# Two Hedgehog stages in one list-scheduled order, PSUM banks given singly, four VectorE passes moved

## The chip, the cores and the metric

The kernel runs on one NeuronCore of a Trainium2 chip. A core has five engines that run side by side, each with its own queue in program order: TensorE (PE, matrix products; its weight loads are listed apart as PEld), VectorE (DVE), ScalarE (ACT), GpSimd (POOL) and SyncE (SP, which here only issues DMAs). They wait for each other on semaphores. Products land in PSUM, 8 banks of 128 x 512 fp32 values. The metric is device time in microseconds, the median of several executions.

## The reference

Four layers on a sequence of 2048 rows of 512, with 32 heads of 16: attention, Hedgehog, attention, Hedgehog, each behind a layer norm and with a residual.

```python
def _A_ref(x, wqkv, wo):
    q, k, v = ...            # x @ wqkv, split in heads
    p = _softmax(einsum("bhqd,bhkd->bhqk", q, k) * Dh ** -0.5)
    return merge(einsum("bhqk,bhkd->bhqd", p, v)) @ wo

def _B_ref(x, wqkv, w_phi, wo):
    q, k, v = ...
    pq, pk = q @ w_phi, k @ w_phi                      # per head
    phi_q = concatenate([_softmax(pq), _softmax(-pq)])  # 32 features
    phi_k = concatenate([_softmax(pk), _softmax(-pk)])
    kv, z = phi_k^T v, sum(phi_k)
    o = (phi_q kv) / (phi_q z + 1e-6)
    return merge(o) @ wo

x = x + _A_ref(_layernorm(x), A_wqkv, A_wo)
x = x + _B_ref(_layernorm(x), B_wqkv, B_w_phi, B_wo)
x = x + _A_ref(_layernorm(x), A_wqkv, A_wo)
x = x + _B_ref(_layernorm(x), B_wqkv, B_w_phi, B_wo)
```

## The kernel before

Everything is one program of straight code. Rows are taken in 16 tiles of 128 (`tt`), four of which are a block `j` of 512. Numbers are held as pairs of fp16 (a high part and a rest), so that a product is three passes (`PASSES`) and a projection of a tile is 12 matmuls of 128 x 512. A layer norm leaves its result transposed in `xnT`.

*Attention* (`LayerA.attention`) is scheduled by a planner of its own, exponentials on ACT being the bound. Its last rows, the third output chunk of block 3 with its residual and layer norm, are a generator, `last_tail`, kept in `self.fill`.

*The feed of a Hedgehog layer* (`LayerB.feed`, called per block at the end of `attention`) is written out by hand. For each tile PE projects keys (`pk`), queries (`pq`) and values (`pbv`), with the transposes of the query features of the tile before (`turn`, L1918) and the key-value product of the tile before (`gather`, L1925) between them. `expo` makes the features' exponents: on VectorE the maximum and minimum per head (L1867, L1868) and two subtractions (L1870, L1871) read PSUM, then ACT takes the exponential (L1872). `part_sums` sums and inverts (L1878, L1879) and scales the keys' inverse by `KS` (L1881), all on VectorE; GpSimd multiplies (L1887). `halves` makes the fp16 pair of the keys (ACT L1893, GpSimd L1894). The values' high part comes from ACT (L1837), their rest from VectorE:

```python
low = lambda: nc.vector.scalar_tensor_tensor(
    vt[:, 1, :, 0:16], pvh, 2.0 ** -8, vt[:, 0, :, 0:16], op0=ALU.mult, op1=ALU.subtract)
```

Steps of `last_tail` are pumped in between the tiles (`self.pumps`), three after each of the first four, then one at a time: L751 (`po`), L754, the layer norm with L561, the transposes L645 (`pst`).

*The flow* (`LayerB.flow`) begins when `blocks` has copied the key-value sums out of PSUM. It is ordered by a list scheduler, `Flow`: tasks are generators that yield an engine and an assumed duration, and the earliest possible one goes next, by rank among those that are due. The ranks of stages and blocks are tables (`RANKS`, and `TAIL` in the last layer). Tasks are `heads` (products L2076, ACT copy L2089, VectorE transposes and division L2095 to L2112, GpSimd rest L2117), `out_block` (L2137, residual add L2140), and, if an attention layer follows, `norm_in` (layer norm), `project` (keys and queries of the next layer's first octet, evacuated by L2234, L2237, L2240), `values` and `bounds` (norm products L1219 and the bound row, `sh`, that the first scores need). A task takes PSUM as a pair of banks (`S` or `W`), or as a single bank of two (`M`).

The attention layer's scores are L1358, and its first one in the second attention layer ends the first Hedgehog stage.

Of the kernel before, what the change touches and what calls it, by code (L numbers as in the profile page):

```python
# [50 lines left out]
GAP = -2  # L51
# [10 lines left out]
RANKS = dict(query=(2,) * 4, heads=(12.4, 3.3, 24, 30.4), out=(10.2, 17.5, 30.6, 25.2), ln=(2.3, -16.8, 14.2, 5.8),  # L62
             keys=(29.8, 57, 32.4, 34.4), project=(59.7, 22.9, -4.7, 53.4), values=(56.3, 0.5, 50, 57.4))
TAIL = dict(query=(5,) * 4, heads=(4.6, 26.6, 16.2, 25.9), out=(11.1, 5.6, 11.5, 25.9))
SOON = ()
# [22 lines left out]

PASSES = ((0, 0), (1, 0), (0, 1))
# [3 lines left out]
def mha_hedgehog_stack(ctx, tc, x_in, a_wqkv, a_wo, b_wqkv, b_wphi, b_wo, out, shmin=SHMIN):  # L93
# [46 lines left out]
    def make_bones():  # L140
        for u in range(4):
            nc.vector.tensor_reduce(bo32[:, u, 8 * u:8 * u + 8], ident.rearrange("p (h d) -> p h d", d=DH), AX.X, ALU.add)
        nc.vector.tensor_copy(bones, bo32)

# [388 lines left out]
    class Norm:  # L533
# [148 lines left out]
        def steps(self):  # L682
            for t in range(4):
                yield
                self.turned(t, 1, psum1("pst").unsqueeze(1))
                if t < 2:
                    self.scaled(t + 2)
            return self.xnT

# [31 lines left out]
    def o_block(j, ob, wo, co, x_src, x_dst, box, after=None, wide=True, early=False, cs=range(NC4)):  # L721


        def load(t2):
# [3 lines left out]
            return xt  # L728

        xt2 = [] if wide else [load(0), load(1)]  # L730
        for t2 in range(2):
            r = (4 * j + 2 * t2) * P
            xt = load(t2) if wide else xt2[t2]
            if wide:
                ps2 = banks("po2")
# [6 lines left out]
            for u in range(0 if early and t2 == 0 else 2):  # L742
                t = 2 * t2 + u
                n = 0
                for c in cs:
                    for a, b in PASSES:
                        if not wide or n % 4 == 0:
                            yield None if n or u + t2 == 0 else GAP
                        if n == 0:
                            ps = ps2[:, u, :] if wide else psum1("po")  # L750
                        nc.tensor.matmul(ps, ob[c][:, a, t * P:(t + 1) * P], wo[:, b, c, :], start=(n == 0), stop=(n == 3 * len(cs) - 1))  # L751
                        n += 1
                if not wide:
                    nc.vector.scalar_tensor_tensor(xt[:, u, :], ps, co, xt[:, u, :], op0=ALU.mult, op1=ALU.add)  # L754
            if wide:
                nc.vector.scalar_tensor_tensor(xt, ps2, co, xt, op0=ALU.mult, op1=ALU.add)
# [126 lines left out]
    class Flow:  # L883

        def __init__(self, **free):
            self.clock = {"T": 0.0, "V": 0.5, "A": 0.5, "P": 0.0}
            self.free, self.tasks, self.count, self.end = free, [], 0, 0.0

        def add(self, gen, rank, ready=0.0):
# [4 lines left out]
            self.pull(t)  # L894

        def pull(self, t):

            while True:
                try:
                    need = next(t.gen)  # L900
                except StopIteration:
                    self.tasks.remove(t)
                    return
                if need[0] == "until":
# [6 lines left out]
                if t.last is not None and t.last != need[0]:  # L911
                    t.ready += 0.25 if t.last == "T" else 0.08
# [10 lines left out]
        def take(self, *names):  # L923
            name = min((name for name in names if self.free[name]), key=lambda name: min(self.free[name]))
            self.free[name].remove(min(self.free[name]))
            return name

        def give(self, name, n=1, wait=0.1):
            self.free[name] += [self.end + wait] * n

        def run(self):

            while self.tasks:
                for t in sorted(self.tasks, key=lambda t: (t.rank, t.seq)):
                    if t.cond is not None:
                        at = t.cond()
                        if at is not None:
                            t.cond, t.ready = None, max(t.ready, at)
                            self.pull(t)
                best = None  # L940
                for e, c in self.clock.items():
                    mine = [t for t in self.tasks if t.need is not None and t.need[0] == e]
                    if not mine:
                        continue
                    due = [t for t in mine if t.ready <= c + HOLD]
                    t = min(due, key=lambda t: (t.rank, t.ready, t.seq)) if due else min(mine, key=lambda t: (t.ready, t.rank, t.seq))
                    at = max(c, t.ready)
# [3 lines left out]
                self.end = self.clock[t.need[0]] = at + t.need[1]  # L951
                t.ready, t.last = self.end, t.need[0]
                t.need = None
                self.pull(t)

    class LayerA:
# [173 lines left out]
        def norm_task(self, G, idx, acc):  # L1130
# [30 lines left out]
            elif j < NJ - 1:  # L1161
                self.more(self.tail(j, dst))
            else:
                self.last = dst
# [4 lines left out]
        def values0(self, j, ps):  # L1169
# [9 lines left out]
            dst = q["v"][:, j * 528:(j + 1) * 528].rearrange("p (x e) -> p x e", e=33)[:, :, 1:33]  # L1179
# [32 lines left out]
        def head_norms(self, i):  # L1212

            psn = psum1("psn")
# [3 lines left out]
            for n, (u, sq) in enumerate(us):  # L1218
                nc.tensor.matmul(psn[0:32, :], bones[:, u], sq, start=(n == 0), stop=(n == len(us) - 1))  # L1219
            nc.vector.tensor_reduce(self.oct[0]["nm"][0:32, i:i + 1], psn[0:32, :], AX.X, ALU.max)  # L1220
# [59 lines left out]
        def head_values(self, j):  # L1280
            self.values0(j, psum1("pv_"))
# [206 lines left out]
        def last_tail(self, j, ob):  # L1488
            xts = []
            ln = Norm(xts, f"a{self.li}_{j}")  # L1490
            yield from o_block(j, {3: ob}, self.wo, con["oA"], self.x_dst, self.x_dst, xts, ln.half, wide=False, cs=(3,))
            for _ in ln.steps():
                yield GAP
            self.out.append(ln.xnT)

# [971 lines left out]
```

## Time and profile before

| | us |
|---|---|
| three runs | 2444.0, 2450.16, 2451.32 |
| median | 2450.16 |
| the profiled execution | 2445.7 |
| its span | 2443.9 |
| first Hedgehog stage: feed, flow | 987.4 to 1163.9, 1163.9 to 1291.0 |
| second Hedgehog stage: feed, flow | 2192.2 to 2366.0, 2366.0 to 2443.9 |
| granted TensorE clock, mean | 0.99 |

In the rows of the profile a time is the start from the beginning of the span, and the number behind it a duration. Durations of neighbouring instructions of an engine overlap by some tens of ns, so that differences of starts are the better price of a row of them. In square brackets stands how long the engine was idle before, and what ended that.

### The profile page before, as it was taken

Reading aid. Unit: us, or ns where it says so; the run is one execution under the profiler, and the core shown is the slowest. Engines: PE = TensorE matmul, PEld = TensorE weight load, DVE = VectorE, ACT = ScalarE, POOL = GpSimd, SP = SyncE. Lnnn points to the kernel's source line nnn. Section 1 sums busy time; section 2 is a strip of 40 time slices with the busy share of each in tenths; the row PEclk is TensorE's granted clock in tenths of the full one; section 3 lists DMA queues with packets and bytes.
Section 4 is the critical chain, followed back from the end, with each engine's and each line's share of the span. In section 5 each row is a group of like instructions: output and inputs, shape, how many; then the busy total and the mean of one; then the engine's idle time right before and its main releaser. Section 6 shows DMA issues by size and latency. Waiting matters only on the chain. (4 is left out here: it accounts for less than half of the span.)

```text
span 2443.9 us, 115599 instructions
## 1 busy us (share of the span) xinstructions
PE 2285.6 (94%) x52586; PEld 1203.6 (49%) x52586; DVE 1900.5 (78%) x3007; ACT 2076.5 (85%) x2323; POOL 326.0 (13%) x476
## 2 busy tenths in 40 slices
PE   6999999999999999889898999999999999998998
PEld 4455555545545554445345554555455444444543
DVE  8567656988786876889974788788978785579897
ACT  6899999999999999444548999999999999984453
POOL 3000000000000000366440000000000000006552
PEclk9999999999999999999999999999999999999999
DMA  5410431233135522010123003303311621210003
GB/s 186 80 22 8 90 64 30 41 44 60 47 78 129 165 89 68 32 35 19 61 72 56 18 19 45 43 4 47 46 49 25 129 86 50 78 65 27 27 1 114
DMA packets 160573, 143.66 MB, mean 59 GB/s; under 512 B 70488, under 2 KB 137672, under 8 KB 159176
## 3 DMA queue, kind: packets, MB, share of 16 engines
q1 hardware_dynamic: 158888, 133.40, 23.1%
q8 instruction: 413, 6.77, 1.2%
q0 software_dynamic: 1184, 2.77, 0.3%
q14 instruction: 88, 0.72, 0.1%
HBM read 62.16 MB, written 41.94 MB: 43 GB/s over the span
## 5 line engine op out<-in xcount | busy, mean ns | idle before, releaser
L1358 PE MATMUL s<-kq 49*32 49x512 f16 x14688 | 771.9, 381 | 65.8 <-DMA kq<-sh 4.5
L1358 PEld LDWEIGHTS <-kq 49*32 49x32 f16 x15872 | 381.0, 89 | 691.8 <-issue 571.4
L1805 PEld LDWEIGHTS <-xnTa 128*128 128x128 f16 x1152 | 110.6, 99 | 157.9 <-DVE f L1871 30.8
L1887 POOL TENSOR_TENSOR f<-f,su 128x1024 f32<-128x1024 f32 x58 | 112.2, 1934 | 492.5 <-DVE su L1881 478.3
L1119 POOL PARTITION_ALL_REDUCE nma<-nmx x6 | 6.3, 1057 | 990.3 <-DVE nmx L1116 990.3
L1364 ACT ACTIVATE p__1008<-s 128x1024 f32<-128x1024 f32 x119 | 127.8, 1074 | 2.9 <-PE s L1358 2.7
L1364 ACT ACTIVATE p__27549<-s 128x1024 f32<-128x1024 f32 x114 | 122.3, 1073 | 2.8 <-PE s L1358 2.6
L1364 ACT ACTIVATE p__27547<-s 128x1024 f32<-128x1024 f32 x109 | 116.9, 1072 | 7.5 <-PE s L1358 7.4
L1364 ACT ACTIVATE p__1011<-s 128x1024 f32<-128x1024 f32 x114 | 122.4, 1074 | 0.0
L1364 ACT ACTIVATE p__27550<-s 128x1024 f32<-128x1024 f32 x112 | 120.2, 1073 | 0.9 <-PE s L1358 0.8
L1364 ACT ACTIVATE p__27548<-s 128x1024 f32<-128x1024 f32 x112 | 120.4, 1075 | 0.3 <-PE s L1358 0.2
L1364 ACT ACTIVATE p__27553<-s 128x1024 f32<-128x1024 f32 x112 | 120.4, 1075 | 0.0
L1364 ACT ACTIVATE p__1007<-s 128x1024 f32<-128x1024 f32 x110 | 118.0, 1073 | 1.3 <-PE s L1358 1.0
L1364 ACT ACTIVATE p__1010<-s 128x1024 f32<-128x1024 f32 x110 | 118.3, 1075 | 0.7 <-PE s L1358 0.6
L1364 ACT ACTIVATE p__1009<-s 128x1024 f32<-128x1024 f32 x108 | 116.3, 1077 | 1.8 <-PE s L1358 1.8
L1364 ACT ACTIVATE p__1013<-s 128x1024 f32<-128x1024 f32 x108 | 115.9, 1074 | 1.3 <-PE s L1358 1.2
L1364 ACT ACTIVATE p__1012<-s 128x1024 f32<-128x1024 f32 x109 | 116.7, 1071 | 0.2
L1872 ACT ACTIVATE f<-f,c_pB 128x1024 f32<-128x1024 f32 x62 | 70.1, 1148 | 51.9 <-DVE f L1871 51.6
L1805 PE MATMUL pbv<-wbv,xnTa 128*128 128x512 f16 x384 | 91.6, 390 | 24.0 <-DVE f L1871 23.9
L1364 ACT ACTIVATE p__1006<-s 128x1024 f32<-128x1024 f32 x103 | 110.8, 1076 | 2.1 <-PE s L1358 1.9
L1364 ACT ACTIVATE p__27552<-s 128x1024 f32<-128x1024 f32 x104 | 111.6, 1073 | 0.3
L1364 ACT ACTIVATE p__27551<-s 128x1024 f32<-128x1024 f32 x104 | 111.4, 1072 | 0.1
(671 smaller groups left out, 7187.0 us busy)
## 6 DMA issues: line engine op xcount, KB each, us to landing
kq<-stg SPq DMA_DIRECT2D x168, 128.0 KB
xd<-xt SPq DMA_DIRECT2D x112, 128.0 KB
xt<-xd SPq DMA_DIRECT2D x80, 128.0 KB
xt<-xd SPq DMA_DIRECT2D x20, 512.0 KB
v<-vyt SPq DMA_DIRECT2D x384, 16.0 KB
oD<-osp SPq DMA_DIRECT2D x48, 128.0 KB
ob<-oD SPq DMA_DIRECT2D x48, 128.0 KB
xd<-xt SPq DMA_DIRECT2D x12, 512.0 KB
```

The costliest lines, as they stand in the source:

```text
L1119: nc.gpsimd.partition_all_reduce(mm, m, P, bass_isa.ReduceOp.max)
L1358: nc.tensor.matmul(banks2[u][32 * c:32 * c + 32, :], self.side(g, half, 64 * u, 0, kt * P + 32 * c, 32), self.side(g, half, 64 * u, 1, j * ...
L1364: nc.scalar.activation(pt, s, AF.Exp, scale=EXPS)
L1805: nc.tensor.matmul(dst, xnT[:, a, c, t * P:(t + 1) * P], w(b, c), start=(i == 0 and c == 0), stop=(i == 2 and c == NC4 - 1))
L1872: nc.scalar.activation(f, f, AF.Exp, scale=con["pB"])
L1887: nc.gpsimd.tensor_tensor(f3, f3, self.part_sums(f3, slice(0, 64), factor), ALU.mult)
```

## The change

The hand-written feed, the pumped tail and the flow become one `Flow` a Hedgehog stage. `attention` ends with its last product; it hands over what its engines still have to do (`self.left`) and the PSUM of its last group (`self.closing`).

- `Flow` keeps eight PSUM banks. A task names what it needs in its step (`"one"` bank, `"two"` neighbours, a buffer), and gets it when the step is placed (`near`, `pick`). Between two steps of a task there is a table of latencies by engines (`LAG`) instead of two numbers.
- `closing` (the last group's normalisation), `tail_out` (the third output chunk of block 3) and `norm_in` for that block are tasks. `key`, `value` and `query` are tasks of a tile, ranked by 9.45 per tile with lags for values, queries and the tail (`LAGS`).
- Four passes leave VectorE: the scaling by `KS` goes to ACT; the values' rest goes to GpSimd, for which ACT first copies the projection to SBUF (`vh2`); the epsilon of the division becomes a bias of the ACT copy of the head products (`con["eps"]`); the evacuation `tq` of the next layer's keys and queries goes to ACT, and its upper clamp to the VectorE pass that follows.
- In the closing, the copy out of PSUM and the fp16 cast go to ACT, the rest to GpSimd. The layer norm's first estimate `y` has a stride of two. The last layer's last output half is added and sent in two pieces, and the order of loads on SP moves with the tasks.

```diff
-RANKS = dict(query=(2,) * 4, heads=(12.4, 3.3, 24, 30.4), out=(10.2, 17.5, 30.6, 25.2), ln=(2.3, -16.8, 14.2, 5.8),
+RANKS = dict(heads=(19.2, -43.8, 20.1, 9.9), out=(50.3, 46.2, 35.8, 25.9), ln=(24.4, -17.8, -49.2, 43.1),
...
+LAGS = (11.7, 21.1, 47), (19.8, 26.5, 34.9)
+TILE = 9.45
...
+    def near(self, wants):
+        at = 0.0
+        for name in wants:
+            if name == "one":
+                x = min(self.banks)
+            elif name == "two":
+                x = min(max(self.banks[b:b + 2]) for b in (0, 2, 4))
+            else:
+                x = min(self.free[name], default=FAR)
+            at = max(at, x)
+        return at
...
-            with tc.manual_schedule(engines=COMPUTE):
-                for j in range(NJ):
...
-                    nxt.feed(j, self.out[j], lambda t: self.pumps(3 if t < 4 else t > 4))
+            self.left = {"T": 0.0, "V": max(0.0, plan.clock["V"] - pe), "A": max(0.0, act - pe), "P": max(0.0, plan.clock["P"] - pe)}
...
+            def key(tt):
+                yield known(blocks, (j, t // 2))
+                b = yield "T", 2.6, "one"
+                project(one(b), tt, lambda b, c: self.wqk[:, 1, b, c, :])
+                f, f3, su = yield from features(one(b), b)
...
+                yield "A", 0.2
+                nc.scalar.activation(su, su, AF.Copy, scale=KS)
...
+                    yield "P", 1.9
+                    nc.gpsimd.tensor_tensor(f3, f3, su.unsqueeze(2).to_broadcast([P, 64, DH]), ALU.mult)
+                    yield "A", 0.97, "p"
+                    nc.scalar.activation(fk[:, 0, :], ff, AF.Copy)
+                    yield "P", 2.08
+                    nc.gpsimd.tensor_tensor(fk[:, 1, :], ff, fk[:, 0, :], ALU.subtract)
...
+                yield known(values, tt)
+                yield "T", 0.74
...
+            def value(tt):
+                    yield "A", 0.5, "yb"
+                    nc.scalar.activation(vh.rearrange("p h d -> p (h d)"), one(b), AF.Copy, scale=2.0 ** -8)
+                    F.give_bank(b)
+                    vt = (yield "A", 0.45, "dep", "vt").tile
+                    nc.scalar.activation(vt[:, 0, :, 0:16], vh, AF.Copy)
+                    yield "P", 1.17
+                    nc.gpsimd.tensor_tensor(vt[:, 1, :, 0:16], vh, vt[:, 0, :, 0:16], ALU.subtract)
...
-                nc.scalar.activation(raw, ps.rearrange("p q t -> p (q t)"), AF.Copy)
+                nc.scalar.activation(raw, two(b).rearrange("p q t -> p (q t)"), AF.Identity, bias=con["eps"])
...
-                nc.vector.tensor_scalar(rec, yt[:, :, :, 16], 1e-6 * KS, None, op0=ALU.add)
-                nc.vector.reciprocal(rec, rec)
+                nc.vector.reciprocal(rec, yt[:, :, :, 16])
...
-                v, y, b = new(), sp.tile([P, 2], F32, name="ly"), sp.tile([P, 2], F32, name="lb")
+                v, y, b = new(), sp.tile([P, 2, 2], F32, name="ly0")[:, :, 0], sp.tile([P, 2], F32, name="lb")
...
-                nc.vector.tensor_scalar(tq, ps, con["qk"], CLAMP, op0=ALU.mult, op1=ALU.min)
+                nc.scalar.activation(tq, one(b), AF.Copy, scale=con["qk"])
...
-                nc.vector.tensor_scalar(hi, tq, -CLAMP, None, op0=ALU.max)
+                nc.vector.tensor_scalar(hi, tq, CLAMP, -CLAMP, op0=ALU.min, op1=ALU.max)
...
+                for tt in range(NT):
+                    F.add(key(tt), TILE * tt)
+                    F.add(value(tt), TILE * tt + FEED["value"])
+                    F.add(query(tt), TILE * tt + FEED["query"])
```

The order on three engines in the first Hedgehog stage, before and after. On VectorE, a tile in the middle of the feed (`pk`, `pq` are the projections in PSUM, `f` the exponents, `su` the sums); before:

```order
L1870 TENSOR_TENSOR f<-pq,mx 128x32x16
L1871 TENSOR_TENSOR f<-mn,pq 128x32x16
L1878 TENSOR_REDUCE su<-f 128x64
L1879 RECIPROCAL su<-su 128x64
L1881 TENSOR_SCALAR su<-su 128x64
L1832 SCALAR_TENSOR_TENSOR vt<-pbv,vt 128x32x16
L1878 TENSOR_REDUCE su<-f 128x64
L1879 RECIPROCAL su<-su 128x64
L1867 TENSOR_REDUCE mx<-pk 128x32
```

And after (`fl` and `fm` are the banks, whatever is in them):

```order
L2098 TENSOR_REDUCE mx<-fm_24198 128x32
L2100 TENSOR_REDUCE mn<-fm_24198 128x32
L2103 TENSOR_TENSOR f<-fm_24198,mx 128x32x16
L2112 TENSOR_REDUCE su<-f 128x64
L2105 TENSOR_TENSOR f<-mn,fm_24198 128x32x16
L2114 RECIPROCAL su<-su 128x64
L2112 TENSOR_REDUCE su<-f 128x64
L2098 TENSOR_REDUCE mx<-fl 128x32
L2114 RECIPROCAL su<-su 128x64
L2100 TENSOR_REDUCE mn<-fl 128x32
```

The scaling and the values' rest are gone, and one projection's sum stands between another's passes. On GpSimd in the feed, before:

```order
L1887 TENSOR_TENSOR f<-f,su 128x1024 x2
L1894 TENSOR_TENSOR fk<-f,fk 128x1024
L1809 MEMSET vt 128x32
L1810 MEMSET vt 128x32
L1887 TENSOR_TENSOR f<-f,su 128x1024 x2
```

And after (L2130 keys, L2204 queries, `vh` the copied values):

```order
L2130 TENSOR_TENSOR f<-f,su 128x1024
L2192 TENSOR_TENSOR vt<-vh_25209,vt 128x32x16
L2135 TENSOR_TENSOR fk<-f,fk 128x1024
L2204 TENSOR_TENSOR f<-f,su 128x1024
L2130 TENSOR_TENSOR f<-f,su 128x1024
L2192 TENSOR_TENSOR vt<-vh_25311,vt 128x32x16
```

The keys' and the queries' multiplications no longer follow each other, and the values' rest stands between them; the two fills of `vt` are made once, ahead of the stage. On TensorE, the first head products of the flow (`qT` and `kvb` make the head products, `ident` and `f` a query tile's transposes); before:

```order
L2076 MATMUL fl<-qT_0_24214,kvb 32x512 x8
L2076 MATMUL double<-qT_0_24214,kvb 32x512 x8
L2076 MATMUL fl<-qT_0_24703,kvb 32x512 x8
L2076 MATMUL double<-qT_0_24703,kvb 32x512 x8
L2076 MATMUL fl<-qT_1_24704,kvb 32x512 x8
L2053 MATMUL pqt<-ident,f 128x128 x4
```

And after:

```order
L2214 MATMUL fm_24199<-ident,f 128x128 x4
L2260 MATMUL fl<-qT_0_24978,kvb 32x512 x8
L2214 MATMUL fm_24199<-ident,f 128x128 x4
L2260 MATMUL fl<-qT_0_24978,kvb 32x512 x8
L2260 MATMUL double<-qT_1_24979,kvb 32x512 x8
L2214 MATMUL fm_24198<-ident,f 128x128 x4
L2260 MATMUL fl<-qT_1_24979,kvb 32x512 x8
L2260 MATMUL fl<-qT_0_24467,kvb 32x512 x8
L2214 MATMUL fm_24199<-ident,f 128x128 x4
L2260 MATMUL double<-qT_0_24467,kvb 32x512 x8
```

Six groups of query transposes, where there were four, stand among the first head products.

More of the change, by code (lines that the diff above doesn't have):

```diff
@@ L49 @@
 FILLED = 112
-GAP = -2
 FAR = 1e9
@@ L727, in load @@
             send(xt, x_src[r:r + 2 * P, :].rearrange("(t p) d -> p t d", p=P))
[L728 to L735, printed above, removed]
+            ps2 = banks("po2")
             if early and t2 == 0:
@@ L910, in pull @@
                     continue
[L911 to L912 removed]
+                e = need[0]
+                t.wants = [x for x in need[2:] if type(x) is str and x != "dep"]
+                t.order = t.rank + sum(x for x in need[2:] if type(x) is float)
+                if t.last is not None and (e != t.last or "dep" in need):
+                    t.ready += LAG[t.last + e]
                 t.need = need
@@ new lines, in key @@
+                    for x in sides:
+                        F.add(side(*x), -1.0, F.end + 0.2)
+                    yield "until", lambda: max(parts) if len(parts) == 2 else None
+                yield known(values, tt)
+                yield "T", 0.74
+                vf = values[(tt, "tile")].rearrange("p a h e -> p a (h e)")
+                for g in range(8):
+                    for n, (a, w) in enumerate(PASSES):
+                        nc.tensor.matmul(W[:, g // 4, (g % 4) * 68:(g % 4) * 68 + 68], fk[:, a, g * P:(g + 1) * P],
+                                         vf[:, w, g * 68:(g + 1) * 68], start=(not gathered and g % 4 == 0 and n == 0),
+                                         stop=(len(gathered) == NT - 1 and n == 2), skip_group_check=True)
@@ L2046, in query @@
+            def query(tt):
+                j, t = divmod(tt, 4)
+                yield known(blocks, (j, t // 2))
+                b = yield "T", 2.6, "one"
+                project(one(b), tt, lambda b, c: self.wqk[:, 0, b, c, :])
+                f, f3, su = yield from features(one(b), b)
+                yield "P", 1.9
                 nc.gpsimd.tensor_tensor(f3, f3, su.unsqueeze(2).to_broadcast([P, 64, DH]), ALU.mult)
                 fq = f.rearrange("p h s f -> p (h s f)")
+                if j not in qTs:
+                    yield F.got(2, "big")
+                    if j not in qTs:
+                        F.take("big"), F.take("big")
+                        qTs[j] = [big([P, 4, 512], F32, f"qT{j}_{i}") for i in range(2)]
@@ L2128, in out_block, with part @@
                 send(xt, self.x_src[r:r + 2 * P, :].rearrange("(t p) d -> p t d", p=P))
-                yield F.got(1, "S", "W")
-                kind, ps2 = pair()
+                end = kind and 2 * j + t2 == 2 * NJ - 1
+                rows = lambda u, n: self.x_dst[r + u * P:r + (u + n) * P, :].rearrange("(t p) d -> p t d", p=P)
+                def part(c, u, ps):
+                    t = 2 * t2 + u
+                    for i, (a, w) in enumerate(PASSES):
+                        nc.tensor.matmul(ps, obs[j][:, c, a, t * P:(t + 1) * P], wo[:, w, c, :],
+                                         start=(c == 0 and i == 0), stop=(c == NC4 - 1 and i == 2))
@@ L2131, in out_block @@
+                if end:
+                    yield known(ready, *[(j, c) for c in range(NC4)])
+                    for u in range(2):
+                        b = yield "T", 2.6, "one"
+                        for c in range(NC4):
+                            part(c, u, one(b))
+                        F.add(out_end(xt[:, u], one(b), b, rows(u, 1)), -1.0, F.end + 0.25)
+                    return
                 for c in range(NC4):
                     yield known(ready, (j, c))
-                    yield "T", 1.3
+                    if c == 0:
+                        b = yield "T", 1.3, "two"
+                    else:
+                        yield "T", 1.3
```

595 lines of the change are left out of this document (350 added, 245 removed).

## Prediction

> **What bounds the kernel now.** I read the page first, then windows by stage, then TensorE's timeline and its waits in the two Hedgehog stages, then the groups of the other engines there. The page's slices:
>
> ```profile
> PE   6999999999999999889898999999999999998998
> DVE  8567656988786876889974788788978785579897
> ACT  6899999999999999444548999999999999984453
> ```
>
> Where ACT stands at 9 attention runs, and the change leaves its instructions in their order. Where ACT falls to 4 and DVE rises to 8 or 9 are the Hedgehog stages, and there PE is below 9. The next view cuts each of them into its feed (projections and features) and its flow (head products, output, the next layer's first octet).
>
> ```profile
> core 0: us, PE busy (x) PEld busy (x) DVE busy (x) ACT busy (x) POOL busy (x), PEclk, DMA share, GB/s
> 987.40:1163.90 176.50, 158.04 (x1108) 83.44 (x1100) 159.05 (x254) 78.96 (x100) 100.47 (x107) 0.99 0.07 25
> 1163.90:1291.00 127.10, 107.08 (x826) 52.17 (x826) 108.86 (x192) 55.55 (x77) 54.02 (x147) 0.95 0.22 65
> 2192.20:2366.00 173.80, 158.14 (x1108) 83.26 (x1100) 157.49 (x252) 78.75 (x100) 100.40 (x105) 0.99 0.06 19
> 2366.00:2443.90 77.90, 65.07 (x465) 23.90 (x464) 62.98 (x100) 29.80 (x41) 22.54 (x18) 0.90 0.26 90
> ```
>
> PE and DVE carry almost the same load (158.0 and 159.1 us in the first feed), so each waits for the other wherever the order is poor. TensorE's timeline gives start, duration, operation, and the idle time before it with its releaser:
>
> ```profile
> 1019.55 2.76 PE L1805 MATMUL pbv<-wbv,xnTa 128*128 128x512 f16 x12 [2.96 <-DVE f L1871]
> ...
> 1023.01 0.81 PE L751 MATMUL po<-woA,osp 128*128 128x512 f16 x3
> ...
> 1113.82 2.75 PE L1805 MATMUL pk<-wbqk,xnTa 128*128 128x512 f16 x12
> 1116.41 2.75 PE L1805 MATMUL pq<-wbqk,xnTa 128*128 128x512 f16 x12
> ...
> 1123.24 2.75 PE L1805 MATMUL pk<-wbqk,xnTa 128*128 128x512 f16 x12
> ```
>
> From one key projection to the next a tile without a gap takes 1123.24 - 1113.82 = **9.42 us**, a projection in it 2.59. Sixteen tiles are 150.7; the attention tail's four output pieces at 0.81 and four groups of transposes at 0.52 (half of the 1.04 below) add 5.3: a feed holds **156** us of PE work. PE's waits in the first stage (total, times, longest) say what makes it 176.5:
>
> ```profile
> PE pbv L1805 <- DVE f L1871: 12.7, 7, 3.0
> PE fl L2137 <- DVE xt L2140: 4.5, 2, 3.6
> PE s L1358 <- DMA kq<-sh: 3.8, 1, 3.8
> ```
>
> The value projection waits for a PSUM bank that VectorE has yet to empty. The flow where it is dense, and both stages' ends:
>
> ```profile
> 1208.84 5.34 PE L2137 MATMUL fl<-wbo,obB 128*128 128x512 f16 x24
> 1214.02 1.04 PE L645 MATMUL fl<-ident,xn 128*128 128x128 f32 x8
> 1214.98 1.09 PE L2076 MATMUL double<-qT,kvb 32*32 32x512 f32 x16
> 1215.55 1.09 PE L2076 MATMUL fl<-qT,kvb 32*32 32x512 f32 x16
> 1216.58 2.85 PE L1176 MATMUL pv__26627<-wAv,xnTb 128*128 128x128 f16 x48
> ...
> 1290.93 1.30 PE L1358 MATMUL s<-kq 49*32 49x512 f16 x16 [3.79 <-DMA kq<-sh]
> 2434.84 1.28 DVE L2140 SCALAR_TENSOR_TENSOR xt<-double,c_oB,xt 128x1024 f32<-128x1024 f32 x1 [3.90 <-PE double L2137]
> ```
>
> By starts an output half-block is 5.18, a transpose pair 0.96, a head product 0.8; the values are 2.85. Eight, eight, sixteen and four of these, eight projections and some 3 us of norm products make 97 of PE work in the first flow; the second, which has only heads and output, has 54. So the first stage is 303.5 us (987.4 to 1290.93) for 253 of matmuls, the second 242.6 (2192.2 to 2434.84) for 210: **about 83 us of PE gaps** are all that an order can win. Behind 2434.84 come the last add and the output's write, 9 us.
>
> **The change part by part.** Groups of the first stage (count, total, mean ns):
>
> ```profile
> L1832 DVE SCALAR_TENSOR_TENSOR vt<-pbv,vt 128x512 f16<-128x512 f32 x16 | 11.0, 685 | 0.8 <-ACT vt L1837 0.8
> L1881 DVE TENSOR_SCALAR su<-su 128x64 f32<-128x64 f32 x16 | 3.1, 195 | 0.6
> L2101 DVE TENSOR_SCALAR rec<-yt 128x32 f32<-128x32 f32 x16 | 5.3, 332 | 0.0
> L2234 DVE TENSOR_SCALAR tq<-double,c_qk 128x512 f32<-128x512 f32 x5 | 3.7, 742 | 2.0 <-PE double L989 2.0
> L1887 POOL TENSOR_TENSOR f<-f,su 128x1024 f32<-128x1024 f32 x29 | 56.1, 1934 | 204.3 <-DVE su L1881 195.6 <-DVE su L1879 5.8 <-PE pbv L1805 2.8
> L1894 POOL TENSOR_TENSOR fk<-f,fk 128x1024 f16<-128x1024 f32 x15 | 32.0, 2133 | 1.2 <-ACT fk L1893 1.2
> L2117 POOL TENSOR_TENSOR obB<-yb,obB 128x512 f16<-128x512 f32 x16 | 18.6, 1171 | 29.5 <-ACT obB L2115 29.5
> L1837 ACT ACTIVATE vt<-pbv 128x512 f16<-128x512 f32 x16 | 9.3, 583 | 1.0 <-PE pbv L1805 1.0
> ```
>
> The four passes: VectorE loses 16 value-low passes (11.0) and 16 scalings (3.1) in a feed, 16 epsilon adds (5.3) in a flow, and eight `tq` evacuations (8 x 0.742 = 5.9) in the first flow. ScalarE gets one more copy (0.58) and one small scaling a tile and eight more copies in the first flow. At 79 busy of 176 and 56 of 127 it hides them; without that cover they would cost up to 16 x 0.8 = 13 a feed. GpSimd gets a 1.17 us pass a tile (priced by `obB`, of the same size): 2 x 1.934 + 2.133 + 1.17 = 7.2 in a tile of 9.42, beside PE. Bounds 0 and 16 x 1.17 = 19 a feed; I take 0, because two other projections now stand between a value projection and the product that needs it.
>
> The tail's integer step (L561, twice a stage) stood behind a GpSimd pass; the same operation elsewhere did not:
>
> ```profile
> 1014.96 2.12 POOL L1894 TENSOR_TENSOR fk<-f,fk 128x1024 f16<-128x1024 f32 x1
> 1015.12 2.00 DVE L561 TENSOR_SCALAR ly<-lu 128x2 int32<-128x2 int32 x1
> 1200.20 0.17 DVE L2168 TENSOR_SCALAR ly<-lu 128x2 int32<-128x2 int32 x1
> ```
>
> It starts while GpSimd works and ends with it, 1.83 us longer than its like. The change writes it with a stride of two. The Trainium skill, SBUF — State Buffer, section Who interferes with whom, says that such a VectorE pass blocks against GpSimd only in a two-port mode, and that one with two SBUF inputs blocks too; the trace agrees for L561 (2.00 against 0.17). [...] My sum needs neither: the rows give it 0 to 3.7 a feed, and I take the middle, 2, since they don't tell whether the place or the form made the difference.
>
> *The feeds.* VectorE's 159.05 becomes 159 - 14.1 - 2 - some 2 for the closing passes that go to other engines = 141, under PE's 156. So a feed becomes PE's, and what is left are a start (VectorE first has closing, residual and layer norm beside the features) and the run-out. Bounds: 156, and 176.5 if nothing comes free. The dense tiles, with 9.1 us of VectorE in 9.42, lie near the lower end already; I take 162.5: **-14 and -11**.
>
> *The flows.* VectorE's 108.86 becomes 108.9 - 5.3 - 5.9 = 98, as much as PE's 97, and 62.98 becomes 57.7 against 54. VectorE was busy 86% of the first flow, and 63 of the 70 us up to the last add, 90%, in the second. At the same density, a little above 86%, the first flow would take 113, the second 64 to 65: **-14 and -5**. The bounds are 98 and 127, 58 and 69. In it are the banks given singly (a projection now takes one, not a pair), the queries that trail the keys by two to four tiles and give PE work while the last keys run, and the octet's start: `s` waited 3.8 for its bound row, and a values product (2.85) now stands behind the third group of norms, which hides most of that. For that start the last projected block is now 2, so its row loads enter the queues of SP and GpSimd just ahead of the bound row; that may give 1 or 2 back.
>
> *The rest.* The last output add in two halves: half of 1.28, -0.6. Two small VectorE passes at the program's start: 0 to 0.7 (two of L2101), 0.3. The output-weight load and the next weights move ahead on SP by tens of us, into feeds whose DMA share is 0.06; nothing waits for them.
>
> Sum: -14 - 11 - 14 - 5 - 0.6 + 0.3 = **-44**. The profiled execution took 2445.7 (span 2443.9); 2445.7 - 44 = 2401.7, and 2402 is my number. The median of the runs is 2450.2, 4.5 above that execution, so an unlucky median would be 2406.
>
> **The rivals.** *The flows give little (A).* With PE and VectorE equal at 97 and 98 us, one late pass stops both, and the transition from the last keys to the first outputs is a chain through all four engines. For it: 4.5 us of waits on `xt` in the old flow. Then only the feeds gain: 2402 + 19 = 2421.
>
> *PE runs nearly closed (B).* With 9 us of gaps left in each stage they take 262 and 219, against 303.5 and 242.6: -65, 2381. For it: the dense tiles. Against it: VectorE would have to be 92% busy throughout, and the clock:
>
> ```profile
> 2370.75 1.96 PE L2076 MATMUL fl<-qT,kvb 32*32 32x512 f32 x16
> ```
>
> A head product took 1.96 there without idle time before it, against 1.09, and the granted clock is 0.90 in that window, 0.95 in the first flow. (1 - 0.95) x 127 + (1 - 0.90) x 78 = 14 us at most. The Trainium skill, TensorE: Matmul & The Clock Gate, section What's actually happening, lets an idle window throttle the clock; by that rule alone closing the gaps would return these 14 and speak for B. The trace agrees only in part, since the row is slow in a run of small products, and the new order has eight head products and six transposes in a row at that place.
>
> *The change doesn't do what it says (C).* The order is fixed beforehand from assumed durations; if they are off, waits move only. Gain under 7: 2442. Against it: the dense tiles of before already run at 9.42.
>
> *GpSimd becomes the bound (D), slower.* Every tile now needs three or four GpSimd passes before its product and transposes, and PE cannot go past a product that waits. At 7.2 of 9.42 it would decide once its passes stretch by more than 1.5: then a tile takes over 11. At 1.7 a tile takes 12.2 and a feed 16 x 12.2 + 5.3 = 200.5, which is 24 and 27 more than now; less the 19 gained in the flows that is +32: 2478. For it: L561 shows that the two engines can stop each other. Against it: 29 passes of 1934 ns mean beside a VectorE that was 90% busy.
>
> **How the numbers follow.** Forecast 0.58 (2385 to 2415), A 0.20, B 0.11, C 0.06, D 0.05. The range leaves out C and D and the far end of B: **2380 to 2428**. About 0.3%, 7 us, is what a measurement can tell from no change. Faster than that 0.89, within it 0.06, slower 0.05.
>
> **What would show it.** Feeds of 160 to 165 us with key projections 9.4 apart from the third tile on; PE's waits for `f` of a few us; GpSimd some 115 to 120 busy in a feed with its passes still at 1.93; `s` waiting under 2. I am wrong if PE waits for GpSimd at the key-value products, if VectorE stays above 150 busy in a feed, or if the flows keep 127 and 69.

## The result, and the profile after

The changed kernel took 2410.98 us (median of four runs, 2408.47 to 2413.07) beside 2447.08 for the kernel before (2443.36 to 2451.32): a ratio of **0.9852, 95% interval 0.9829 to 0.9874**, 36 us less where 44 were forecast. The profiled execution took 2411.36 us, with a span of 2409.5. The busy tenths of its page, engine by engine:

```profile
PE   6999999999999999988999999999999999999998
DVE  8567656888687877787974698789877876569887
ACT  6899999999999999655658999999999999995663
```

TensorE's row is below 9 only in two slices between the program's ends, in the first Hedgehog stage; the second shows none. The windows by feed and flow of the changed kernel (columns as before: stretch, length, busy time of each engine, granted clock, DMA share, GB/s):

```profile
core 0: us, PE busy (x) PEld busy (x) DVE busy (x) ACT busy (x) POOL busy (x), PEclk, DMA share, GB/s
986.40:1162.30 175.90, 159.51 (x1104) 84.56 (x1096) 139.94 (x214) 91.48 (x132) 114.22 (x94) 0.98 0.07 25
1162.30:1273.50 111.20, 103.77 (x829) 51.99 (x829) 92.36 (x167) 62.65 (x86) 53.59 (x147) 0.98 0.25 74
2176.10:2336.40 160.30, 156.02 (x1105) 83.97 (x1097) 141.34 (x212) 91.55 (x132) 113.56 (x92) 0.99 0.07 21
2336.40:2409.50 73.10, 59.99 (x468) 23.49 (x468) 56.52 (x84) 30.80 (x42) 22.61 (x18) 0.96 0.28 96
```

By the starts in the trace, the 34.4 us between the two spans are: first feed 176.5 to 175.9 (**-0.6, forecast -14**), first flow 127.0 to 111.15 (-15.9, forecast -14), second feed 173.8 to 160.3 (-13.5, forecast -11), second flow with the tail 77.9 to 73.1 (-4.8, forecast -5.6), an earlier start of the first stage (-1.0) and a slower second attention (+1.3).

So one term is missing, though VectorE's load fell in the first feed as it did in the second: 159.1 to 139.9, and 157.5 to 141.3. The second feed runs as forecast; TensorE's timeline there has one tile's pair of key and query projections start 2280.83 - 2271.41 = 9.42 us behind the other's:

```profile
2271.41 5.34 PE L2026 MATMUL fm<-wbqk,xnTa 128*128 128x512 f16 x24
...
2280.83 2.54 PE L2026 MATMUL fm<-wbqk,xnTa 128*128 128x512 f16 x11
```

In the first feed the projections that follow a tile's first transposes start at 1108.19, 1119.47 and 1130.75 there, 11.28 us apart. What TensorE waited for, and then ScalarE (engine, tile and line, releaser: total us, times, longest; TensorE's window reaches over the flow too):

```profile
PE double L2164 <- POOL vt L2192: 6.3, 6, 1.9
PE fl L2026 <- DVE mx L2098: 2.8, 2, 2.3
...
PE fl L2214 <- POOL f L2204: 2.0, 3, 0.7
```

```profile
ACT f L2108 <- DVE f L2105: 27.6, 17, 7.7
ACT qT L2216 <- PE fl L2026: 17.3, 6, 3.3
```

TensorE's list points at GpSimd's new pass, `vt` L2192, in front of the key-value product, which is the sign that the prediction had named for being wrong. That was the first theory. The second list has a row that is odd in itself: a copy of the transposed queries (L2216) released by a *projection* (L2026), which it doesn't read.

### The profile page after: what moved, and what is told of

Its sections match the earlier page's. It is cut to its first block, busy times and chain, and to the rows that moved or that the text cites. A ratio compares the mean times of both kernels' runs of the same rounds, so it can differ in the third digit from the quotient of the medians.

```text
span 2409.5 us, 115540 instructions
## 1 busy us (share of the span) xinstructions
PE 2274.7 (94%) x52586; PEld 1204.7 (50%) x52586; DVE 1845.2 (77%) x2892; ACT 2109.9 (88%) x2395; POOL 354.7 (15%) x462
## 4 chain that ended last, share of the span: by engine, by line
ACT 41%; PE 31%; DVE 14%; issue 9%; POOL 2%; DMA 1%; SPq 0%; ACTq 0%; DVEq 0%; POOLq 0%
PE s L1390 6%; PE double L1436 6%; PE pm L1436 5%; PE fl L2026 3%; PE fm L2026 3%; ACT p__1011 L1396 3%; ACT p__1012 L1396 2%; ACT p__1014 L1396 2%; ACT p__1010 L1396 2%; ACT p__1016 L1396 2%; ACT p__1013 L1396 2%; ACT p__27393 L1396 2%; ACT p__27398 L1396 2%; ACT p__27396 L1396 2%; ACT p__27392 L1396 2%
## 5 line engine op out<-in xcount | busy, mean ns | idle before, releaser
L2026 PEld LDWEIGHTS <-xnTa 128*128 128x128 f16 x1152 | 112.3, 99 | 132.9 <-issue 13.6
L1396 ACT ACTIVATE p__1011<-s 128x1024 f32<-128x1024 f32 x119 | 127.8, 1074 | 2.5 <-PE s L1390 2.3
L1396 ACT ACTIVATE p__27392<-s 128x1024 f32<-128x1024 f32 x114 | 122.3, 1073 | 2.4 <-PE s L1390 2.4
L1396 ACT ACTIVATE p__1014<-s 128x1024 f32<-128x1024 f32 x114 | 122.4, 1074 | 0.2 <-PE s L1390 0.2
L1396 ACT ACTIVATE p__27390<-s 128x1024 f32<-128x1024 f32 x109 | 116.9, 1073 | 6.1 <-PE s L1390 6.0
L1396 ACT ACTIVATE p__27393<-s 128x1024 f32<-128x1024 f32 x112 | 120.2, 1073 | 1.7 <-PE s L1390 1.5
L1396 ACT ACTIVATE p__27391<-s 128x1024 f32<-128x1024 f32 x112 | 120.5, 1076 | 0.4 <-PE s L1390 0.2
L1396 ACT ACTIVATE p__27396<-s 128x1024 f32<-128x1024 f32 x112 | 120.6, 1077 | 0.2 <-PE double L751 0.2
L1396 ACT ACTIVATE p__1010<-s 128x1024 f32<-128x1024 f32 x110 | 118.1, 1073 | 1.3 <-PE s L1390 1.0
L1396 ACT ACTIVATE p__1013<-s 128x1024 f32<-128x1024 f32 x110 | 118.0, 1073 | 0.7 <-PE s L1390 0.6
L1396 ACT ACTIVATE p__1012<-s 128x1024 f32<-128x1024 f32 x108 | 116.2, 1076 | 2.3 <-PE s L1390 2.3
L1396 ACT ACTIVATE p__1015<-s 128x1024 f32<-128x1024 f32 x109 | 116.7, 1071 | 1.0 <-PE s L1390 0.8
L1396 ACT ACTIVATE p__1016<-s 128x1024 f32<-128x1024 f32 x108 | 115.8, 1072 | 0.4 <-PE s L1390 0.4
L2026 PE MATMUL fm<-wbqk,xnTa 128*128 128x512 f16 x492 | 111.6, 379 | 1.4 <-DVE f L2105 1.3
L1396 ACT ACTIVATE p__1009<-s 128x1024 f32<-128x1024 f32 x103 | 110.7, 1075 | 1.8 <-PE s L1390 1.6
L1396 ACT ACTIVATE p__27395<-s 128x1024 f32<-128x1024 f32 x104 | 111.4, 1072 | 0.3
L1396 ACT ACTIVATE p__27394<-s 128x1024 f32<-128x1024 f32 x104 | 111.5, 1072 | 0.2 <-PE s L1390 0.2
L1396 ACT ACTIVATE p__27398<-s 128x1024 f32<-128x1024 f32 x101 | 108.5, 1074 | 0.1
```

The source lines that it names most:

```text
L1396: nc.scalar.activation(pt, s, AF.Exp, scale=EXPS)
L2026: nc.tensor.matmul(ps, xnT[:, a, c, t * P:(t + 1) * P], w(b, c), start=(i == 0 and c == 0), stop=(i == 2 and c == NC4 - 1))
```

## Experiments

Stage lengths of every run (us, from the starts in each profiled execution's trace), the median, and the ratio to runs of the kernel before on the same chip with its 95% interval. A feed reaches from its first projection to the first head product, the first flow from there to the attention's first scores, the second to the end of the span:

| run | feed 1 | flow 1 | attention | feed 2 | flow 2 + tail | median | ratio |
|---|---|---|---|---|---|---|---|
| before | 176.5 | 127.0 | 901.3 | 173.8 | 77.9 | 2447.1 | 1 |
| changed | 175.9 | 111.2 | 902.7 | 160.3 | 73.1 | 2411.0 | 0.9852 (0.9829-0.9874) |
| e1_norest | 175.5 | 110.8 | 902.0 | 158.9 | 72.3 | 2410.7 | 0.9847 (0.9831-0.9863) |
| e2_rest_vector | 183.3 | 112.4 | 903.4 | 171.5 | 73.1 | 2430.7 | 0.9928 (0.9911-0.9945) |
| e3_lags_one | 174.3 | 110.5 | 903.8 | 160.3 | 72.4 | 2408.6 | 0.9841 (0.9820-0.9862) |
| e4_direct | 183.8 | 115.7 | 902.5 | 188.0 | 71.7 | 2449.8 | 1.0003 (0.9988-1.0019) |
| e5_other_pair | 162.9 | 110.9 | 903.7 | 158.9 | 72.4 | 2402.6 | 0.9823 (0.9806-0.9840) |
| e6_apart | 155.9 | 111.2 | 903.1 | 159.1 | 76.3 | 2392.8 | 0.9777 (0.9760-0.9793) |
| e7_apart_direct | 160.1 | 116.5 | 900.6 | 164.6 | 72.9 | 2403.0 | 0.9821 (0.9804-0.9837) |
| e8_pair_norest | 165.7 | 110.8 | 902.5 | 158.9 | 73.3 | 2400.6 | 0.9814 (0.9796-0.9833) |
| e9_eps_tq | 155.9 | 116.6 | 903.6 | 159.1 | 75.5 | 2400.6 | 0.9809 (0.9793-0.9826) |
| e10_ks | 159.9 | 112.6 | 904.9 | 158.0 | 76.1 | 2401.0 | 0.9796 (0.9783-0.9809) |
| e11_no_stride | 175.9 | 111.2 | 902.7 | 160.3 | 72.2 | 2410.4 | 0.9846 (0.9831-0.9861) |
| e12_old_lags | 160.5 | 115.2 | 902.8 | 162.4 | 74.4 | 2405.6 | 0.9815 (0.9793-0.9837) |

A stage's length is that of one execution. The attention, which no edit touches, takes 900.6 to 904.9, and the first feed starts between 983.3 (e7) and 988.8 (e10). So verdicts on a stage are read from its own column. A stage that an edit leaves alone repeats there within 0.1 us at best (first feed 155.9 in e6 and e9) and within 1.4 at worst (second feed 160.3 in the changed kernel and 158.9 in e5).

### Is it GpSimd's new pass?

**e1_norest** takes the suspect out, so the values keep only their high part:

```
-                nc.gpsimd.memset(vt[:, 1, :, 16:17], 0.0)
+                nc.gpsimd.memset(vt[:, 1, :, :], 0.0)
...
-                    nc.gpsimd.tensor_tensor(vt[:, 1, :, 0:16], vh, vt[:, 0, :, 0:16], ALU.subtract)
```

> GpSimd's pass for the values' rest is left out in both feeds (the rests are zero, so the values are rounded to 16 bits); all other instructions keep their order on every engine. Theory 1 (the order: the pass stands in GpSimd's queue behind the keys' scaling, which waits for ScalarE's small scaling, and the key-value product waits for it): the 6.3 us of product waits for GpSimd go and with them most of the wide tiles (11.28 us each from 1097 to 1140); first feed from 175.9 to 162-168, second stays at 159-161, 2397-2404 us in all. Theory 2 (GpSimd's load): both feeds fall, the first by 10 or more, the second by 2 or more, since GpSimd's busy time falls from 114 to 95 in each. Theory 3 (VectorE, whose 140 us in a feed wait for ScalarE and PE in turn): nothing that can be measured, first feed 174-177.

First feed 175.5. The waits for `vt` are gone, GpSimd has 96.7 us in place of 114.2, and the tiles still stand 11.3 apart; the transposes now wait for `f` instead (0.86 in place of 0.68 in each). Theory 1, as far as it is about this pass, and theory 2 fall. TensorE's longest wait was what came last, not what it depended on.

**e2_rest_vector** moves the same instruction to VectorE, at its place:

```
-                    nc.gpsimd.tensor_tensor(vt[:, 1, :, 0:16], vh, vt[:, 0, :, 0:16], ALU.subtract)
+                    nc.vector.tensor_tensor(vt[:, 1, :, 0:16], vh, vt[:, 0, :, 0:16], ALU.subtract)
```

> The values' rest is computed by VectorE, at the place in the order at which GpSimd computed it; TensorE's, ScalarE's and GpSimd's other instructions keep their order. Theory 1 (GpSimd's queue holds the pass back): the product's waits for GpSimd's vt go, first feed 163-170, second 160-164 since VectorE, with 141 + 11 = 152 us in a feed of 160, has little left. Theory 2 (GpSimd's load): first feed 162-168, second 158-160. Theory 3 (VectorE limits): both feeds grow by 5 to 11 us each, 2420-2432 us in all.

Feeds 183.3 and 171.5: +7.5 and +11.2, as theory 3 had it. That VectorE's room is narrow in this order is shown; why the first feed is long at equal VectorE load is not.

**e3_lags_one** orders the first feed as the second:

```
-LAGS = (11.7, 21.1, 47), (19.8, 26.5, 34.9)
+LAGS = (19.8, 26.5, 34.9), (19.8, 26.5, 34.9)
```

> The first feed is ordered by the second's lags (values 19.8, queries 26.5 and attention tail 34.9 in place of 11.7, 21.1 and 47); no operation is added or removed. Theory 1 (order): the values come most of a tile earlier against their product, the product's waits for GpSimd fall below 2 us, first feed 160-165, and the whole 2396-2402 us unless the flow behind it gives some back. Theory 2 (GpSimd's load) and theory 3 (VectorE's): the load of each engine is as before, so the first feed stays at 172-178 and the whole at 2408-2414.

174.3. Theory 1 falls in this form too: with the same distances that take 160.3 in the second stage, the first stays long, as theories 2 and 3 had it. VectorE's waits in this feed have another odd row:

```profile
DVE mx L2098 <- PE fl L2026: 8.1, 4, 3.0
DVE mn L2100 <- PE fl L2026: 2.8, 1, 2.8
```

`mn` reads the same bank as the `mx` pass before it, so its own projection had ended long before.

**e4_direct** gives the pass back as it was before the change, with a new order for it:

```
-DIRECT = ()
+DIRECT = tuple(range(16))
```

> The values' rest goes back to VectorE straight from PSUM, as before the change, in all 32 tiles (the copy to a 32-bit tile goes too), and the order is made anew for it. Theory 1 (order and GpSimd's place in it): first feed 162-170, second 160-166, as VectorE has 152 us in it. Theory 2 (GpSimd's load): both feeds below 163. Theory 3 (VectorE's load made the feeds long, and its relief is what the second feed gained): second feed back at 168-174, first at 174-180, 2418-2430 us in all.

2449.8, the whole gain lost and outside the range of every theory, and the second feed 188.0 us: 14 longer than in the kernel before, though VectorE has 148.4 us in it and had 157.5 before. VectorE's load doesn't explain that. Its VectorE waits in the second feed:

```profile
DVE f L2105 <- PE fl L2026: 9.6, 4, 2.8
DVE f L2103 <- PE fl L2026: 5.7, 2, 2.9
```

`f` L2105 and L2103 read a bank that `mx` and `mn` have read already, and are released by a projection all the same.

### The two banks of one tile

The rows fit one thing. `fl` is a tile of two PSUM banks, given singly by the change. One wide tile (11.28 us) of the changed kernel, without the rows of VectorE (start, duration, engine, line, operation, idle time before it and its releaser):

```profile
1118.98 0.66 PE L2214 MATMUL fl<-ident,f 128*128 128x128 f32 x4 [0.68 <-POOL f L2204]
1119.47 2.75 PE L2026 MATMUL fl<-wbqk,xnTa 128*128 128x512 f16 x12
...
1122.27 0.60 ACT L2216 ACTIVATE qT<-fl 128x512 f32<-128x512 f32 x1 [3.33 <-PE fl L2026]
...
1122.76 0.25 ACT L2126 ACTIVATE su<-su 128x64 f32<-128x64 f32 x1
...
1123.09 1.94 POOL L2130 TENSOR_TENSOR f<-f,su 128x1024 f32<-128x1024 f32 x1 [4.16 <-ACT su L2126]
...
1126.15 0.84 PE L2164 MATMUL double<-vt,fk 128*128 128x68 f16 x22 [0.83 <-POOL vt L2192]
```

The transposes into one bank of `fl` end at 1119.6. TensorE goes on with a projection into the *other* bank, and ScalarE's copy of the transposes starts when that projection ends, at 1122.2. Everything behind the copy in ScalarE's queue comes late: the keys' small scaling, GpSimd's scaling (idle 4.16), its value pass, and so the product. In the trace the transposes raise no semaphore of their own: the one that the copy waits for is raised by the projection's last matmul. Six copies of the first feed start so (17.3 us of waits), and two `mn` passes near its start:

```profile
DVE mn L2100 <- PE fl L2026: 8.2, 2, 5.4
```

In the second feed a copy and a feature pass do (2.2 and 1.7 us). The Trainium skill, Perfetto Trace Analysis, section Matmuls, says that independent matmul groups should rotate through different banks so that the evacuation of one overlaps the next group's matmuls; here the banks differed, and six evacuations still waited 17.3 us for the next group's matmuls, because the two banks were one tile.

**e5_other_pair** changes only which bank is taken, from the sixth tile of the first feed on; every engine's order stays:

```
-                    got = min(free, key=lambda b: (b < 6 and self.banks[b ^ 1] <= at, b < 6, self.banks[b]))
+                    got = min(free, key=lambda b: (b < 6 and (self.banks[b ^ 1] > at if self.spread else self.banks[b ^ 1] <= at), b < 6, self.banks[b]))
...
                 gathered.append(F.end)
+                F.spread = 5 <= len(gathered) < NT and not kind
```

> From the sixth tile of the first feed on, a one-bank tile is taken from a pair of banks whose other bank is idle, where the changed kernel takes it from a pair whose other bank is in use; nothing is added, removed or moved in any engine's order, and the second stage is as it was. Six query copies of ScalarE no longer share a two-bank tile with the projection that TensorE runs behind the transposes. Theory 4 (a copy out of one bank waits for a projection into the other bank of the same tile, 2.4 to 3.5 us each, and ScalarE's queue behind it holds GpSimd and the product): the six copies start within 0.1 us of their transposes or of ScalarE's last instruction, the tiles from 1050 on are 9.4 to 10 us apart, first feed from 175.9 to 160-168, second 160, 2395-2404 us in all. Theory 1' (the distance in the order, not the banks): the copies wait as before, first feed 174-177, 2409-2413 us.

162.9: **-13.0 us in the first feed** from the choice of banks alone, as theory 4 had it. The same place in its timeline (line numbers are up to two higher):

```profile
1106.67 0.91 PE L2165 MATMUL double<-vt,fk 128*128 128x68 f16 x24
...
1110.01 0.60 PE L2216 MATMUL fl<-ident,f 128*128 128x128 f32 x4
...
1110.20 0.60 ACT L2189 ACTIVATE vh<-fm 128x512 f32<-128x512 f32 x1 [1.71 <-PE fm L2027]
1110.44 2.75 PE L2027 MATMUL fl<-wbqk,xnTa 128*128 128x512 f16 x12
1110.70 0.59 ACT L2218 ACTIVATE qT<-fl 128x512 f32<-128x512 f32 x1
...
1111.66 1.94 POOL L2131 TENSOR_TENSOR f<-f,su 128x1024 f32<-128x1024 f32 x1 [2.28 <-ACT su L2127]
...
1116.06 0.91 PE L2165 MATMUL double<-vt,fk 128*128 128x68 f16 x24
```

The copy runs beside the projection, which now goes to the other `fl`, and key-value products are 1116.06 - 1106.67 = 9.39 apart. Theory 1' falls. The two `mn` passes stand before the sixth tile and still wait, 5.7 us in all.

**e6_apart** takes banks so through both feeds (the last line of the diff is then `F.spread = len(gathered) < NT`, from the start on), and the order follows:

> The same choice of banks through both feeds, and the order follows it. Theory 4: the waits for the other bank go from nine to one in the first feed and from two to none in the second; first feed 158-167, second 157-161, 2392-2403 us in all. Theory 1': first feed 173-178, second 159-163, 2407-2415 us. Against both: pairs come free later, the attention tail's pieces wait for them, and the first tiles lose 2 to 5 us.

2392.8, the fastest of all. Feed 1 155.9, which is 20.0 less than in the changed kernel, 7.0 less than in e5 and below theory 4's 158 to 167. The two `mn` waits are gone, and one wait for the other bank is left:

```profile
ACT qT L2218 <- PE fl L2027: 2.4, 1, 2.4
```

TensorE is busy for 153.8 of the 155.9 us. How much of the 7.0 comes from the early waits and how much from the new order wasn't taken apart. The second flow is 3.9 longer than in e5, at a granted clock of 0.84 against 0.96; why stays open. Of the 9.8 us between the two medians the profiled executions hold 3.6, since e5's was the fastest of its four, 5.9 below its median.

**e7_apart_direct** is e4 with the banks chosen apart:

> The values' rest back on VectorE in all tiles, straight from PSUM, with the banks chosen apart as in the run before it. If the 2450 us of the same undoing with shared pairs came from waits for the other bank (eleven and ten of them), the feeds fall to 165-172 each and the whole to 2410-2425 us; what is left against the run before it (some 5 to 10 us a feed) is the worth of the moved pass. If they came from VectorE's load, the feeds stay at 180-188 and the whole at 2440-2450 us.

2403.0 in place of 2449.8: 47 us between two kernels of the same passes on the same engines, by the banks and the order that follows from them. The feeds, 160.1 and 164.6, came out below the 165 to 172 expected. What the moved pass is worth in them is the rest against e6: 4.2 in the first, 5.5 in the second. The medians are 10 apart, but that holds more: the first flow is 5.3 longer too, at a granted clock of 0.91 against 0.98, though the pass has no part in it.

**e8_pair_norest** is e5 without GpSimd's value pass, as in e1:

> The first run of this set, and GpSimd's pass for the values' rest left out as well (the rests are zero). With the query copies free, this says whether the product's wait for that pass was a cost of its own: if so, first feed 3 to 7 us below the first run of this set; if it was only what came last behind the held-up copy, the same within 2 us, in the second feed too.

Feeds 165.7 and 158.9 against 162.9 and 158.9. The first is 2.8 longer without the pass, and the second is the same: with the copies free no cost of the pass shows either.

### The smaller passes

All on e6's order but e11. **e9_eps_tq**:

```
-                nc.scalar.activation(raw, two(b).rearrange("p q t -> p (q t)"), AF.Identity, bias=con["eps"])
+                nc.scalar.activation(raw, two(b).rearrange("p q t -> p (q t)"), AF.Copy)
...
-                nc.vector.reciprocal(rec, yt[:, :, :, 16])
+                nc.vector.tensor_scalar(rec, yt[:, :, :, 16], 1e-6 * KS, None, op0=ALU.add)
+                nc.vector.reciprocal(rec, rec)
...
-                nc.scalar.activation(tq, one(b), AF.Copy, scale=con["qk"])
+                nc.vector.tensor_scalar(tq, one(b), con["qk"], None, op0=ALU.mult)
```

> From the run with the banks apart (2392.8 us), with every other instruction in its place: the epsilon goes back to VectorE as a pass of its own (16 x 0.33 = 5.3 us in each flow) and so do the eight tq evacuations (8 x 0.75 = 6 in the first flow). If the flows' gain came from VectorE's relief, as the prediction's share of it says (5.3 + 5.9 of 14 and all 5 of the second), the first flow grows by 5 to 11 and the second by 2 to 5, 2400-2408 us in all. If it came from the one order and the banks given singly, with VectorE idle a quarter of the flow (88 of 112), the flows grow by less than 2 each, 2391-2397.

The windows of the first feed and flow of e6, and then the flow's of e9:

```profile
985.80:1141.70 155.90, 153.83 (x1105) 83.48 (x1098) 141.11 (x214) 91.72 (x132) 114.22 (x94) 1.00 0.08 28
1141.70:1252.80 111.10, 103.68 (x828) 51.98 (x829) 92.24 (x167) 62.57 (x86) 53.62 (x147) 0.98 0.25 74
```

```profile
1142.20:1258.80 116.60, 102.78 (x828) 50.97 (x829) 101.85 (x191) 56.44 (x78) 52.97 (x147) 1.00 0.24 70
```

VectorE has 9.6 us more, ScalarE 6.1 less, and the flow is 5.5 longer, while the first feed and the second are as they were. That is the low end of the 5 to 11 that VectorE's relief would be worth in the first flow. The second flow, where only the epsilon moves, is 0.8 shorter, so no worth shows there. All this is at e6's order; whether an order made for these passes would lose less wasn't tried. The whole is 8 us above e6, and 5.8 in the profiled executions.

**e10_ks**:

```
-                nc.scalar.activation(su, su, AF.Copy, scale=KS)
+                nc.vector.tensor_scalar(su, su, KS, None, op0=ALU.mult)
```

> From the run with the banks apart, all else in its place: the small scaling of the keys' sums goes back from ScalarE to VectorE (16 x 0.195 = 3.1 us in each feed). If VectorE bounds the feeds, each grows by 2 to 4 us, 2396-2401 in all. If ScalarE's queue held the keys back (the scaling waits there behind an exponential or a copy, and GpSimd's scaling of the keys waits for it), the feeds shrink by 1 to 3 each, 2387-2391. If PE bounds them, within 2 us of 2392.8.

Feed 1 is 4.0 longer, as if VectorE bounded it, and feed 2 is 1.1 shorter, with the same edit in both. The two don't agree, and this stays open. Nor does the whole's 8 us decide: of the 9.0 us between the two profiled executions, 3.0 are a later start of the first feed and 1.8 the attention.

**e11_no_stride**, on the changed kernel:

```
-                v, y, b = new(), sp.tile([P, 2, 2], F32, name="ly0")[:, :, 0], sp.tile([P, 2], F32, name="lb")
+                v, y, b = new(), sp.tile([P, 2], F32, name="ly"), sp.tile([P, 2], F32, name="lb")
```

> The changed kernel with the integer step's output without a stride, as before the change; all else in its place. If the stride frees the step from GpSimd's pass, the two of each feed that now take 0.17 to 1.85 us all take about 2, and the whole grows by 0 to 4 us. If only the place decides (the changed kernel's strided step still took 1.78 and 1.85 us where a GpSimd pass of 1.95 and 1.93 ran beside it), the durations are the same within 0.2 us each and the time stays within 2 us of the changed kernel's 2411.

The integer step of the changed kernel with its stride, in the first and the second feed, with the GpSimd pass beside the first:

```profile
1031.28 1.95 POOL L2204 TENSOR_TENSOR f<-f,su 128x1024 f32<-128x1024 f32 x1 [0.61 <-DVE mv L2364]
1031.48 1.78 DVE L2368 TENSOR_SCALAR ly<-lu 128x2 int32<-128x2 int32 x1
...
2204.05 1.85 DVE L2368 TENSOR_SCALAR ly<-lu 128x2 int32<-128x2 int32 x1
...
2215.15 0.17 DVE L2368 TENSOR_SCALAR ly<-lu 128x2 int32<-128x2 int32 x1
```

And without it:

```profile
1030.33 1.78 DVE L2368 TENSOR_SCALAR ly<-lu 128x2 int32<-128x2 int32 x1
...
2203.17 1.86 DVE L2368 TENSOR_SCALAR ly<-lu 128x2 int32<-128x2 int32 x1
...
2214.34 0.17 DVE L2368 TENSOR_SCALAR ly<-lu 128x2 int32<-128x2 int32 x1
```

The same within 0.01, and the whole is 2410.4 against 2411.0. The place decides.

**e12_old_lags**:

```
-LAG = dict(TV=0.25, TA=0.25, TP=0.25, TT=0.0, VT=0.15, VA=0.13, VP=0.26, VV=0.13, AV=0.18, AP=0.2, AT=0.15, AA=0.13, PA=0.05, PT=0.06, PV=0.1, PP=0.05)
+LAG = {a + b: 0.25 if a == "T" else 0.08 for a in "TVAP" for b in "TVAP"}
```

> From the run with the banks apart: the planner reckons a hand-over at 0.25 us from TensorE and 0.08 from every other engine, as before the change, in place of the table by pairs; no operation changes, the order is made anew. If the table is what makes the new order good, the feeds and flows grow by 3 to 6 us in sum or more, 2398-2410. If it hardly matters beside the banks and the single list, within 3 us of 2392.8.

The whole is 13 us above e6, and the four stages hold 512.5 against 502.5: 4.6 and 3.3 more in the feeds, 4.0 more in the first flow, 1.9 less in the second. That is the first expectation: the order made with the table by pairs is the better one, by some 10 us of stages. The ranks were kept; whether other ranks would win this back with the old numbers wasn't tried.

## Why the prediction was right, and where not

The forecast of 2402 lies 9 us under the median, which is inside 2380 to 2428. Its steps:

- **"So a feed becomes PE's, and what is left are a start ... and the run-out"** is the step that failed, and in the first feed alone. The size taken, 162.5, was enough where the banks aren't shared: the first feed is 162.9 in e5 and 155.9 in e6, at the lower bound of 156; the second feed of the changed kernel, with two such waits, is 160.3. The sum lacked a term for a new wait that the change itself made: a bank given singly out of a two-bank tile ties its reader to the matmuls in the other bank. It cost 13.0 us there (e5), or 20.0 with the order that follows the banks (e6), and it couldn't be read from the trace of before, where the transposes had tiles of their own. The prediction counted "the banks given singly" as a gain only.
- **GpSimd's added pass at 0** was right, in size and against its upper bound of 19: e1 and e8 take it away and gain 0.4 and -2.8 us in the first feed. The test set for it was a bad one: TensorE did wait for GpSimd at the product, six times for 6.3 us, and the waits were worth nothing. Nor did rival D's stretch come: GpSimd's passes kept 1.93, and it was 114 busy, just under the 115 to 120 named.
- **The flows at 113 and 64 to 65** came out at 111.2 and 64.2 (up to the last add). The working scaled VectorE's load by its density, and that is borne out in part: with the epsilon and `tq` passes back on VectorE the first flow grows by 5.5 us and the second doesn't (e9), so VectorE's relief is about a third of the first flow's 15.9 and none that shows of the second's 4.6. What is left is the one order, the banks given singly and the clock; these weren't taken apart.
- **VectorE's relief in the feeds** is real but smaller than its load: the value pass is 11.0 us of VectorE and 4.2 and 5.5 us of feed (e7 against e6). The small scaling is 3.1 us, and the two feeds disagree on it (4.0 more and 1.1 less in e10).
- **The integer step at 2 us a feed** was 0 for its form (e11). The 2 us came all the same, by place and so by luck: one of the two steps of a feed fell where no GpSimd pass ran and took 0.17, and the other waited as before, for 1.78 and 1.85 (3.9 us for both in a feed before, 2.0 now).
- **`s` under 2**: 2.17 (3.79 before). **The last add**: 0.75 in place of 1.28, as forecast.
- Rival B's clock came in part: 0.95 and 0.90 in the flows of before are 0.98 and 0.96 now. Priced as the prediction priced it, at most, that is (0.05 x 127) - (0.02 x 111) = 4 us of the first flow's gain and (0.10 x 78) - (0.04 x 73) = 5 of the second's, an estimate that no run here tested. Rivals A and C are out by the flows and the second feed.
- That the whole came so near has luck in it. The first feed missed by 13.4 us, and the second feed and the first flow gave 2.5 and 1.9 more than forecast; the range, 48 us wide, had room for the rest and would have held rival A's 2421 too.

## What to carry to other kernels

A wait list says what came last at an engine, not what it hung on; look in the queues of the engines behind it for a row whose releaser is not its own data, and take the named pass away before believing in it. When PSUM banks of a wider tile are handed out one by one, choose neighbours that aren't in use at the same time, or give single users tiles of their own: here that was worth 13.0 us of one feed, more than a moved pass was worth in any stage (5.5 for the value pass, 5.5 for the epsilon and `tq` together). Judge such an edit in its own stage, since the untouched attention took 900.6 to 904.9 us and the first feed's start moved by 5.

## What the runs showed of the hardware

- ScalarE reads one PSUM tile while TensorE writes another at full pace (e5: the copy 0.59 us long beside a 2.75 us projection). Whether the chip would also allow it for the two banks of one tile wasn't tried, since the wait is in the program.
- The integer step, a VectorE pass on 128x2 elements, takes 1.78 to 1.86 us in place of 0.17 when it starts just after a GpSimd pass of 1.9 us, and ends with it, with a stride in its output or without (e11). The Trainium skill, VectorE: DVE Perf Modes, section What auto-detection actually checks, makes the two-port mode hang on where source and destination lie and on the counts of their outermost dimensions, and names a step only for the packed 16-bit mode; the two runs agree with it (1.85 us with the stride, 1.86 without).
